# Second MoE of a fused attention and MoE kernel: three slots on the first weight buffer, two weight splits moved to VectorE, two products ahead of the next transposes

## The chip, the cores and the metric

The kernel runs on one core of a Trainium2 chip. The core has five engines, each with its own instruction queue that it works through in order: TensorE (PE) for matrix products, with its weight loads shown apart as PEld, VectorE (DVE), ScalarE (ACT), GpSimd (POOL) and SyncE (SP), which here issues most of the transfers. The engines wait for one another through semaphores. The metric is the time of one execution on the device, in microseconds (us).

## The reference

Three layers follow each other: an attention over 2 x 8 heads of 768 tokens, a dense two-layer network with a leaky activation, and a routed mixture of eight experts, which is the part that the change touches:

```
logits = x @ w_gate + modality_bias[modality_id]      # 1536 tokens, 512 wide, 8 experts
e_idx = np.argmax(logits, axis=1)
gate_w = probs[np.arange(N), e_idx]                   # softmax of logits at e_idx
for e in range(E):
    mask = e_idx == e
    if not mask.any():
        continue
    h = np.maximum(x[mask] @ w1[e], 0.0)              # 512 -> 1024
    out[mask] = gate_w[mask, None] * (h @ w2[e])      # 1024 -> 512
```

Each token goes through one expert only, and which one is known only when the layer before is done.

## The kernel before, in words

The attention and the first network run under a planner that records the operations and issues them in an order of its own; they fill the first 410 us or so. The second MoE, from `first()` on (line 1205), is issued in the order in which the code is written.

**Slots.** The tokens are sorted by expert into tiles of at most 128, called slots. There can be up to 19 slots; the kernel runs as many as are needed. The slots of one expert stand together. The first expert is the one with most tokens in the first two thirds, chosen early (`early_route`, with its weights fetched early), and the others follow by number. `exi` holds, for each slot, the expert and a flag that says whether new weights are needed.

**Weights.** One expert's weights are 4 MB in eight chunks: 0 to 3 are w1, 4 to 7 are w2. A chunk of 512 KB comes into one of seven `raw` tiles by a transfer that SyncE issues (`fetch_w`), and is then split into a rounded part, copied by ScalarE, and the rest, subtracted by VectorE (`split_w`, line 976; chunks 4 and 7 of slot 0 have the rest taken on GpSimd, line 1208 and 1218). Products use three of the four pairs of parts, so each is three matmuls. There are two weight buffers `mw`. `buf(t)` (line 960) gives slot 0 and slot 1 the first, slot 2 the second, and so on by turns. A slot needs new weights if its expert differs from that of the slot that had the same buffer two slots earlier; slot 2 is always the first in its buffer, so its flag is always set. For slot 1, whose expert may differ from slot 0's though they share the buffer, `other_weights_1` (line 1282) holds a conditional block that reloads the buffer in halves through small tiles `z`.

**The order of a slot.** `mm1(t, c)` is the first layer for a quarter of the columns (twelve matmuls, then a ReLU copy `hs` on ScalarE); `h_T(t, c)` transposes `hs` on TensorE and splits it into `ht` (ScalarE, then VectorE); `mm2(t, c)` is the second layer for the same quarter (six matmuls); `x_T(t)` transposes a slot's gathered rows `xg` and splits them into `xs`. After the fourth `mm2`, VectorE scales the result to `y` and GpSimd scatters it. `period(t)` runs a slot with the last two `mm2` of the slot before mixed in, and with conditional blocks (`split_if`) that split the next slot's chunks, each followed by the fetch of as many chunks further ahead (`fetch_more`).

**Routing.** `first()` runs slot 0 with the routing steps between: `route_a` (before it) builds, on VectorE, the one-hot tables `ma` and `mj`; `route_b` multiplies them on TensorE and gives `gidx`, by which GpSimd gathers the rows of slots 1 and 2; `route_c` and `route_d` give `exi`. The two halves of slot 1's conditional block then stand on either side of `mm2(0, 3)`.

Of the kernel before, what the change touches and what calls it, by code (L numbers as in the profile page):

```python
# [17 lines left out]
ALU = mybir.AluOpType  # L18
# [263 lines left out]
def tile_kernel(  # L282
# [5 lines left out]
    nc = tc.nc  # L288
    plan = Plan(tc)
    V, S, G, T, Y = (  # L290
        plan.engine(e, c) for e, c in ((nc.vector, "D"), (nc.scalar, "A"), (nc.gpsimd, "G"), (nc.tensor, "P"), (nc.sync, "S"))
    )
# [3 lines left out]
    E = w_gate.shape[1]  # L296
# [26 lines left out]
    def bank(pool, tag):  # L323
        return pool.tile([P, 512], F32, tag=tag, name=tag)
# [441 lines left out]
    NS = NTT + E  # L766
# [42 lines left out]
    exi = const.tile([P, 2 * NS + 2], I32, name="exi")  # L809
# [99 lines left out]
    def route_b():  # L909
        mj = rt["mj"]  # L910
        sp = bank(ps_a, "a")
        for t in range(NTT):
            T.matmul(out=sp[:, 0:NS], lhsT=mas[t], rhs=mj[:, t], start=(t == 0), stop=(t == NTT - 1))
        V.tensor_scalar(out=gidx, in0=sp[:, 0:NS], scalar1=-1.0, scalar2=0.0, op0=ALU.add, op1=ALU.max)
        fetch_x(1, gidx[:, 1:2])
        fetch_x(2, gidx[:, 2:3])
        rt["sp"] = sp
# [18 lines left out]
    def route_d():  # L936
        exs, ns, be, sp = (rt[n] for n in ("exs", "ns", "be", "sp"))
        V.tensor_scalar(out=exs[:, 1], in0=colf[:, 0:NS], scalar1=ns, scalar2=esf, op0=ALU.is_lt, op1=ALU.mult)
        V.scalar_tensor_tensor(out=exs[:, 0], in0=colf[:, 0:NS], scalar=ns, in1=exs[:, 0], op0=ALU.is_ge, op1=ALU.mult)
        V.tensor_tensor(out=exs[:, 0], in0=exs[:, 0], in1=exs[:, 1], op=ALU.add)  # L940
        V.tensor_scalar(out=exi[:, 0:NS], in0=exs[:, 0], scalar1=float(E - 1), scalar2=None, op0=ALU.min)
        V.memset(exs[:, 2, 0:3], 1.0)
        V.tensor_tensor(out=exs[:, 2, 1:2], in0=exs[:, 0, 1:2], in1=exs[:, 0, 0:1], op=ALU.not_equal)
        V.tensor_tensor(out=exs[:, 2, 3:], in0=exs[:, 0, 3:], in1=exs[:, 0, 1:NS - 2], op=ALU.not_equal)

        V.scalar_tensor_tensor(out=exi[:, NS:2 * NS], in0=colf[:, 0:NS], scalar=be[:, 1, E - 1:E], in1=exs[:, 2], op0=ALU.is_lt, op1=ALU.mult)
        V.tensor_copy(out=exi[:, 2 * NS:2 * NS + 1], in_=be[:, 1, E - 1:E])
        sidf = lt.tile([P, NS], F32, name="sidf")
        V.tensor_scalar(out=sidf, in0=sp[:, 0:NS], scalar1=0.5, scalar2=float(4 * NT), op0=ALU.is_lt, op1=ALU.mult)
        V.scalar_tensor_tensor(out=sidx, in0=sp[:, 0:NS], scalar=-1.0, in1=sidf, op0=ALU.add, op1=ALU.add)  # L950


    EN_SP = [mybir.EngineType.SP]
    EN_AV = [mybir.EngineType.Activation, mybir.EngineType.DVE]
# [3 lines left out]
    raw_of = {}  # L958

    def buf(t):  # L960
        return 0 if t == 0 else (t - 1) % 2

    def fetch_w(t, e, cond, c):
        raw = rawt[nraw[0] % len(rawt)]
# [11 lines left out]
    def split_w(t, chunks, eng=V):  # L976
        for c in chunks:
            raw, hl = raw_of.pop((t, c)), mw[buf(t)][c]
            S.activation(out=hl[:, 0], in_=raw, func=ACTF.Copy)
            eng.tensor_tensor(out=hl[:, 1], in0=raw, in1=hl[:, 0].bitcast(F32), op=ALU.subtract)  # L980
# [8 lines left out]
    def spl(dst, src):  # L989
        S.activation(out=dst[:, 0], in_=src, func=ACTF.Copy)  # L990
        V.tensor_tensor(out=dst[:, 1], in0=src, in1=dst[:, 0].bitcast(F32), op=ALU.subtract)
# [166 lines left out]
    def mm1(t, c):  # L1158
        hp = bank(ps_h, "h")
        xt = xs_t[t % 2]  # L1160
        wv = mw[buf(t)][c].rearrange("p t (k f) -> p t k f", k=KD)
        n = 0
        for kk in range(KD):
            for xa, wa in P3:
                T.matmul(out=hp[:, 0:QW], lhsT=xt[:, xa, kk, :], rhs=wv[:, wa, kk, :], start=(n == 0), stop=(n == 3 * KD - 1))
                n += 1
        hs = gp.tile([P, QW], F32, tag="t", name="hs")
        S.activation(out=hs, in_=hp[:, 0:QW], func=ACTF.Relu)
        sl[t, "h", c] = hs

    def h_T(t, c):
        hs = sl.pop((t, "h", c))
        tp = bank(ps_a, "a").rearrange("p (a c) -> p a c", a=KD)
        for a in range(2):
            T.transpose(tp[:, a], hs[:, a * P:(a + 1) * P], ident)
        ht = gp.tile([P, 2, 2, P], F32R, tag="g", name="ht")
        spl(ht, tp[:, 0:2])
        sl[t, "ht", c] = ht

    def mm2(t, c):  # L1180
        if c == 0:
            sl[t, "y"] = bank(ps_acc, "acc")
        ht, yp = sl.pop((t, "ht", c)), sl[t, "y"]
        wv = mw[buf(t)][4 + c].rearrange("p t (k f) -> p t k f", k=2)
        for k2 in range(2):
            for j, (ha, wa) in enumerate(P3):
                T.matmul(
                    out=yp, lhsT=ht[:, ha, k2, :], rhs=wv[:, wa, k2, :],
                    start=(c == 0 and k2 == 0 and j == 0), stop=(c == 3 and k2 == 1 and j == 2),
                )  # L1190
        if c == 3:
            y = p2.tile([P, DM], F32, tag="y", name="y", bufs=2)
            V.tensor_scalar(out=y, in0=sl.pop((t, "y")), scalar1=gcol[:, t:t + 1], scalar2=None, op0=ALU.mult)
            G.indirect_dma_start(
                out=out, out_offset=bass.IndirectOffsetOnAxis(ap=sidx[:, t:t + 1], axis=0), in_=y, in_offset=None,
                bounds_check=NT - 1, oob_is_err=False,
            )

    def next_x(u):
        if u < NS - 1:  # L1200
            x_T(u)
        if u + 1 < NS - 1:
            fetch_x(u + 1, gidx[:, u + 1:u + 2])

    def first():
        mm1(0, 0)
        mm1(0, 1)
        split_w(0, [4], G)
        h_T(0, 0)
        split_w(0, [5])  # L1210
        mm1(0, 2)
        h_T(0, 1)
        mm1(0, 3)
        route_b()
        split_w(0, [6])
        mm2(0, 0)
        h_T(0, 2)
        split_w(0, [7], G)
        route_c()
        mm2(0, 1)  # L1220
        h_T(0, 3)
        route_d()
        x_T(1)
        mm2(0, 2)
        other_weights_1(range(4))
        mm2(0, 3)
        other_weights_1(range(4, 8))
        fetch_more(7)

    def period(t, lagged):  # L1230

        u = t + 1
        mm1(t, 0)
        if lagged:
            mm2(t - 1, 2)
        next_x(u)
        split_if(t, [6])
        mm1(t, 1)
        h_T(t, 0)
        split_if(t, [7])  # L1240
        split_if(u, [0])
        if lagged:
            mm2(t - 1, 3)
        mm1(t, 2)
        h_T(t, 1)
        split_if(u, [1, 2])
        mm2(t, 0)
        mm1(t, 3)
        h_T(t, 2)
        split_if(u, [3, 4])  # L1250
        mm2(t, 1)
        h_T(t, 3)
        split_if(u, [5])

    def drain(t):
        mm2(t, 2)
        mm2(t, 3)

    fq = [(u, c) for u in range(2, NS - 1) for c in range(8)]
    regs = {}  # L1260

    def fetch_more(n):
# [9 lines left out]
            fetch_w(u, *regs[u], c)  # L1272

    def split_if(u, chunks):
        if not 2 <= u < NS - 1:
            return
        need = nc.values_load(exi[0:1, NS + u:NS + u + 1], engines=EN_AV, min_val=0, max_val=1)  # L1277
        with tc.If(need > 0):
            split_w(u, chunks)
        fetch_more(len(chunks))  # L1280

    def other_weights_1(chunks):

        e = nc.values_load(exi[0:1, 1:2], engines=EN_SP, min_val=0, max_val=E - 1)
        need = nc.values_load(exi[0:1, NS + 1:NS + 2], engines=EN_AV + EN_SP, min_val=0, max_val=1)
        with tc.If(need > 0):  # L1286
            for c in chunks:
                for j in range(2):
                    z = p2.tile([P, 512], F32, tag="y", name="z", bufs=2)
                    if c < 4:  # L1290
                        Y.dma_start(out=z.rearrange("p (e k f) -> p e k f", e=1, k=2), in_=w1v[:, ds(e, 1), 2 * j:2 * j + 2, c * QW:(c + 1) * QW])
                    else:
                        Y.dma_start(out=z.rearrange("p (e d) -> p e d", e=1), in_=w2v[:, ds(e, 1), 2 * (c - 4) + j, :])
                    hl = mw[0][c][:, :, j * 512:(j + 1) * 512]
                    S.activation(out=hl[:, 0], in_=z, func=ACTF.Copy)
                    V.tensor_tensor(out=hl[:, 1], in0=z, in1=hl[:, 0].bitcast(F32), op=ALU.subtract)
# [9 lines left out]
    e = nc.values_load(exi[0:1, 2 * NS + 1:2 * NS + 2], engines=EN_SP, min_val=0, max_val=E - 1)  # L1306
# [48 lines left out]
```

## Time and profile before

| | us |
|---|---|
| median of three runs | 627.63 |
| lowest and highest | 626.22, 629.51 |
| the profiled execution, device time | 628.37 |
| its span in the trace | 626.6 |
| TensorE busy | 571.8 (91%) |
| VectorE busy | 388.4 (62%) |
| ScalarE busy | 307.2 (49%) |
| GpSimd busy | 214.7 (34%) |

The span is the time from the first to the last recorded instruction; the device time has a little more around it. A row of a timeline gives the start, the length of the merged run of equal instructions, the engine, what is written and what is read, how many, and in square brackets the idle time of the engine before it with what ended it. Line L70 is the helper that issues every operation outside the planner, so rows are told apart by tile names: h is mm1's result, acc mm2's, and a the one that all transposes and small products share. The ends of matmuls are modelled and overlap a little; in the chain of waits the overlaps are taken out.

### The profile page before, as it was taken

The numbers are of one execution on the slowest core, as the hardware profiler recorded it, in microseconds if no ns is written. First come the engines' busy times: TensorE is split into PE (matmuls) and PEld (weight loads), VectorE is DVE, ScalarE is ACT, GpSimd is POOL, SyncE is SP. The second block draws the span as 40 slices with busy tenths as digits, with TensorE's granted clock in tenths as the row PEclk, the third lists the DMA queues.
The fourth block names the chain that finished last, engine by engine and source line by source line (L and its number), as shares of the span: only waits on it lengthen the run. The fifth ranks groups of instructions, "written<-read, shape, count | busy, mean of one in ns | idle before, by whom it ended". The sixth has DMA issues, their size and how long they took to land. (4 is left out here: it accounts for less than half of the span.)

```text
span 626.6 us, 13126 instructions
## 1 busy us (share of the span) xinstructions
PE 571.8 (91%) x4476; PEld 511.5 (82%) x4476; DVE 388.4 (62%) x1005; ACT 307.2 (49%) x653; POOL 214.7 (34%) x221
## 2 busy tenths in 40 slices
PE   4568798999979999999999999997699999999995
PEld 3457687888869898998998999886599999998994
DVE  7899889878547777777322433878452249982221
ACT  3765667767535454453332343543442258872231
POOL 3445547355125456465322222215011211121120
PEclk9868879999979999999999999999899999999999
DMA  9897999896423233222000000552811199941111
GB/s 185 181 197 150 215 188 182 152 177 110 89 72 82 88 102 102 72 96 68 1 2 2 34 35 35 190 169 80 299 40 34 53 317 336 360 171 51 36 53 34
DMA packets 119856, 75.82 MB, mean 121 GB/s; under 512 B 87355, under 2 KB 107863, under 8 KB 119768
## 3 DMA queue, kind: packets, MB, share of 16 engines
q1 hardware_dynamic: 117208, 67.14, 42.5%
q0 software_dynamic: 2560, 7.64, 3.9%
q8 instruction: 39, 0.64, 0.4%
q14 instruction: 49, 0.40, 0.2%
HBM read 97.08 MB, written 7.30 MB: 167 GB/s over the span
## 5 line engine op out<-in xcount | busy, mean ns | idle before, releaser
L153 PE MATMUL h<-xT,w 128*128 128x256 f32 x888 | 117.6, 288 | 1.9 <-ACT xT L153 1.5
L153 PEld LDWEIGHTS h<-xT,w 128*128 128x128 f32 x888 | 113.6, 194 | 5.1 <-ACT xT L153 1.7
L153 PE MATMUL acc<-w,g 128*128 128x512 f32 x432 | 110.7, 404 | 4.2 <-ACTq L1090 4.2
L70 PE MATMUL h<-mw,xs 128*128 128x256 f32 x720 | 99.2, 287 | 0.4 <-DVEq L1286 0.4
L153 POOL TENSOR_TENSOR g<-t,g 128x256 fp32r<-128x256 f32 x74 | 65.0, 881 | 98.8 <-ACT g L153 58.2
L70 PE MATMUL acc<-mw,ht 128*128 128x512 f32 x360 | 96.8, 406 | 0.3 <-DVE ht L70 0.3
L153 PEld LDWEIGHTS acc<-w,g 128*128 128x128 f32 x432 | 80.3, 193 | 20.4 <-ACTq L1090 4.5
L70 PEld LDWEIGHTS h<-mw,xs 128*128 128x128 f32 x720 | 92.6, 192 | 3.4 <-DVEq L1286 0.7
L70 PEld LDWEIGHTS acc<-mw,ht 128*128 128x128 f32 x360 | 63.5, 188 | 12.0 <-DVE ht L70 0.8
L70 POOL DMA_INDIRECT out<-y,sidx x15 | 18.4, 1225 | 152.7 <-DVE y L70 138.2
L70 DVE TENSOR_TENSOR mw<-raw,mw 128x1024 fp32r<-128x1024 f32 x46 | 55.4, 1224 | 14.8 <-ACT mw L70 13.8
L153 DVE SCALAR_TENSOR_TENSOR t<-t,alpha_sb,h 128x256 f32<-128x256 f32 x74 | 35.2, 477 | 45.2 <-ACT t L153 45.1
L153 POOL TENSOR_TENSOR w<-dx,w 128x512 fp32r<-128x512 f32 x32 | 43.6, 1361 | 53.0 <-ACT w L153 50.1
L70 ACT ACTIVATE hs<-h 128x256 f32<-128x256 f32 x60 | 22.8, 380 | 68.5 <-PE h L70 61.0
L70 ACT ACTIVATE mw<-raw 128x1024 fp32r<-128x1024 f32 x48 | 49.6, 1055 | 13.9 <-DMA raw<-in_moe_w 10.2
L153 DVE SCALAR_TENSOR_TENSOR dx<-wraw,dx 128x512 uint32<-128x512 uint32 x64 | 53.3, 837 | 0.4
L70 DVE TENSOR_TENSOR ht<-a,ht 128x256 fp32r<-128x256 f32 x60 | 25.2, 421 | 45.4 <-ACT ht L70 45.4
L153 ACT ACTIVATE t<-h 128x256 f32<-128x256 f32 x74 | 28.0, 381 | 43.8 <-PE h L153 42.0
L153 ACT ACTIVATE g<-t 128x256 fp32r<-128x256 f32 x74 | 30.8, 418 | 36.4 <-DVE t L153 31.3
L153 ACT ACTIVATE sp<-sp,mn 128x256 f32<-128x256 f32 (+1 forms) x96 | 39.4, 479 | 15.7 <-DVE mn L153 15.7
L153 PE MATMUL a<-vring,pth 128*128 128x64 bf16 (+1 forms) x880 | 36.2, 203 | 8.1 <-DMA pth<-pl 6.8
L153 PEld LDWEIGHTS <-pth 128*128 128x128 f16 x880 | 32.5, 104 | 12.5 <-DMA pth<-pl 7.7
(167 smaller groups left out, 835.0 us busy)
## 6 DMA issues: line engine op xcount, KB each, us to landing
raw<-in_moe_w SPq DMA_DIRECT2D x125, 512.0 KB
wraw<-in_moe_w_in SPq DMA_DIRECT2D x16, 512.0 KB
wraw<-in_moe_w_out SPq DMA_DIRECT2D x16, 512.0 KB
xs<-x SPq DMA_DIRECT2D x12, 258.0 KB
kr<-in_k SPq DMA_DIRECT2D x12, 256.0 KB
qr<-in_q SPq DMA_DIRECT2D x12, 256.0 KB
vr<-in_v SPq DMA_DIRECT2D x12, 256.0 KB
vring<-vglob SPq DMA_DIRECT2D x8, 96.5 KB
```

The source lines that it names most:

```text
L70: return method(*a, **kw)
L153: call = lambda: method(*a, **kw)
```

## The change

Slots 0, 1 and 2 have the first buffer, and later slots take the second and the first by turns. `route_d` sets the flags to fit: slots 1 and 2 are compared with the slot just before, slot 3 is always flagged, later ones are compared two slots back. `other_weights` now takes the slot as an argument, and its two halves for slot 2 stand at the end of `period(1)` and, in `period(2)`, behind `mm2(1, 3)`. The queue of fetches and the splits begin with slot 3. In `first()` the subtractions for chunks 4 and 7 are on VectorE, and `mm2(0, 2)`, which is two products of three matmuls each, stands ahead of `route_d` and `x_T(1)`.

```diff
-        V.memset(exs[:, 2, 0:3], 1.0)
-        V.tensor_tensor(out=exs[:, 2, 1:2], in0=exs[:, 0, 1:2], in1=exs[:, 0, 0:1], op=ALU.not_equal)
-        V.tensor_tensor(out=exs[:, 2, 3:], in0=exs[:, 0, 3:], in1=exs[:, 0, 1:NS - 2], op=ALU.not_equal)
+        V.memset(exs[:, 2, 0:4], 1.0)
+        V.tensor_tensor(out=exs[:, 2, 1:3], in0=exs[:, 0, 1:3], in1=exs[:, 0, 0:2], op=ALU.not_equal)
+        V.tensor_tensor(out=exs[:, 2, 4:], in0=exs[:, 0, 4:], in1=exs[:, 0, 2:NS - 2], op=ALU.not_equal)
...
     def buf(t):
-        return 0 if t == 0 else (t - 1) % 2
+        return 0 if t < 3 else t % 2
...
     def first():
         mm1(0, 0)
         mm1(0, 1)
-        split_w(0, [4], G)
+        split_w(0, [4])
         h_T(0, 0)
...
-        split_w(0, [7], G)
+        split_w(0, [7])
         route_c()
         mm2(0, 1)
         h_T(0, 3)
+        mm2(0, 2)
         route_d()
         x_T(1)
-        mm2(0, 2)
-        other_weights_1(range(4))
+        other_weights(1, range(4))
         mm2(0, 3)
-        other_weights_1(range(4, 8))
+        other_weights(1, range(4, 8))
         fetch_more(7)
...
     def period(t, lagged):
...
         if lagged:
             mm2(t - 1, 3)
+            if t == 2:
+                other_weights(2, range(4, 8))
...
         split_if(u, [5])
+        if t == 1:
+            other_weights(2, range(4))
...
-    fq = [(u, c) for u in range(2, NS - 1) for c in range(8)]
+    fq = [(u, c) for u in range(3, NS - 1) for c in range(8)]
...
     def split_if(u, chunks):
-        if not 2 <= u < NS - 1:
+        if not 3 <= u < NS - 1:
             return
...
-    def other_weights_1(chunks):
+    def other_weights(t, chunks):
-        e = nc.values_load(exi[0:1, 1:2], engines=EN_SP, min_val=0, max_val=E - 1)
-        need = nc.values_load(exi[0:1, NS + 1:NS + 2], engines=EN_AV + EN_SP, min_val=0, max_val=1)
+        e = nc.values_load(exi[0:1, t:t + 1], engines=EN_SP, min_val=0, max_val=E - 1)
+        need = nc.values_load(exi[0:1, NS + t:NS + t + 1], engines=EN_AV + EN_SP, min_val=0, max_val=1)
```

How the queues change is seen at three places. The first is VectorE in the routing, from mj on; mw_4 to mw_7 are the rests of slot 0's w2 chunks, and pre, be, nst and ex are route_c's. Before:

```order
L70 TENSOR_TENSOR mj<-jrel,jf 128x240
L70 TENSOR_TENSOR ht<-a,ht 128x256
L70 TENSOR_TENSOR mw_5_6979<-raw_5964,mw_5_6979 128x1024
L70 TENSOR_TENSOR ht<-a,ht 128x256
L70 TENSOR_SCALAR gidx<-a 128x20
L70 TENSOR_TENSOR mw_6_6980<-raw_5962,mw_6_6980 128x1024
L70 TENSOR_TENSOR ht<-a,ht 128x256
L70 TENSOR_TENSOR pre<-before,tl 128x64
```

On the same engine at the same place after the change:

```order
L70 TENSOR_TENSOR mj<-jrel,jf 128x240
L70 TENSOR_TENSOR mw_4_6978<-raw_5963,mw_4_6978 128x1024
L70 TENSOR_TENSOR ht<-a,ht 128x256
L70 TENSOR_TENSOR mw_5_6979<-raw_5964,mw_5_6979 128x1024
L70 TENSOR_TENSOR ht<-a,ht 128x256
L70 TENSOR_SCALAR gidx<-a 128x20
L70 TENSOR_TENSOR mw_6_6980<-raw_5962,mw_6_6980 128x1024
L70 TENSOR_TENSOR ht<-a,ht 128x256
L70 TENSOR_TENSOR mw_7_6981<-raw_6982,mw_7_6981 128x1024
L70 TENSOR_TENSOR pre<-before,tl 128x64
```

Two subtractions have come in, one ahead of the first ht and so of gidx, one ahead of route_c and so of exi.

The second place is ScalarE behind slot 1's first transposes; hs and ht belong to slot 1, and mw_0 to mw_2 with numbers from 6986 on are slot 2's chunks in the second buffer. Before:

```order
L70 ACTIVATE hs<-h 128x256
L70 ACTIVATE ht<-a 128x256
L1277 TENSOR_LOAD exi
L1277 ISA x2
L1278 COMPARE_AND_BRANCH
L70 ACTIVATE mw_0_6986<-raw_6983 128x1024
L1278 UNCONDITIONAL_BRANCH x2
L70 ACTIVATE hs<-h 128x256
L70 ACTIVATE ht<-a 128x256
```

On ScalarE there after the change, up to the block that now stands ahead of slot 2 (z are the small tiles of the reload):

```order
L70 ACTIVATE hs<-h 128x256
L70 ACTIVATE ht<-a 128x256
L70 ACTIVATE hs<-h 128x256
L70 ACTIVATE ht<-a 128x256
L70 ACTIVATE hs<-h 128x256
L70 ACTIVATE ht<-a 128x256 x2
L1289 TENSOR_LOAD exi
L1290 COMPARE_AND_BRANCH
L70 ACTIVATE mw_0_5956<-z 128x512 x2
```

The weight copies between slot 1's own copies are gone, and the conditional block for slot 2 stands behind slot 1's last ht.

The third place is VectorE in slot 2 after the change; y is slot 1's result, mw_0_6986 the first chunk of slot 3, and the block at L1289 the second half of slot 2's:

```order
L70 TENSOR_TENSOR ht<-a,ht 128x256
L1281 TENSOR_LOAD exi
L1282 COMPARE_AND_BRANCH
L70 TENSOR_TENSOR mw_0_6986<-raw_6983,mw_0_6986 128x1024
L1282 UNCONDITIONAL_BRANCH x2
L70 TENSOR_SCALAR y<-acc,gcol 128x512
L1289 TENSOR_LOAD exi
L1290 COMPARE_AND_BRANCH
L70 TENSOR_TENSOR mw_4_6978<-z,mw_4_6978 128x512 x2
```

The block that guards the w2 half of the first buffer stands behind y, and y behind a split.

## Rows read from the trace of the kernel before

**Rows 1.** Stretches: us, each engine's busy us (instructions), TensorE clock, DMA share, GB/s.

```profile
430.00:460.00 30.00, 22.63 (x138) 19.74 (x139) 17.22 (x31) 13.40 (x22) 5.22 (x4) 0.94 0.54 180
450.00:453.00 3.00, 1.84 (x9) 1.85 (x10) 2.72 (x4) 2.74 (x5) 0.00 (x0) 0.62 1.00 367
460.00:490.00 30.00, 30.00 (x201) 27.18 (x200) 8.38 (x18) 8.01 (x22) 5.95 (x6) 1.00 0.16 51
```

**Rows 2.** Chain that ended last, around 440 to 458: start, length, what.

```profile
440.16 9.59 DMA raw<-in_moe_w
...
451.84 2.49 PE h L70 x12
...
456.18 1.43 PE h L70 x12
457.61 0.22 PE a L70 x2
457.83 1.39 PE acc L70 x6
```

**Rows 3.** Timeline of TensorE, 424 to 452: start, length, what, idle before.

```profile
424.85 0.46 PE L70 MATMUL a<-mj,ma 128*128 128x20 f16 x12 [1.39 <-DVE mj L70]
...
431.08 0.63 PE L70 MATMUL a<-ident,xg 128*128 128x128 f32 x4 [2.43 <-DMA xg<-xs,gidx]
...
435.04 1.55 PE L70 MATMUL h<-mw,xs 128*128 128x256 f32 x11 [0.42 <-DVEq L1286]
...
441.51 1.58 PE L70 MATMUL h<-mw,xs 128*128 128x256 f32 x12
444.38 0.44 PE L70 MATMUL a<-ident,hs 128*128 128x128 f32 x2 [1.29 <-ACT hs L70]
...
451.16 0.69 PE L70 MATMUL a<-ident,hs 128*128 128x128 f32 x2 [4.26 <-ACT hs L70]
```

**Rows 4.** Timeline of ScalarE, at slot 2's first weight chunk.

```profile
442.99 1.06 ACT L70 ACTIVATE mw<-raw 128x1024 fp32r<-128x1024 f32 x1 [3.83 <-DMA raw<-in_moe_w]
```

**Rows 5.** Tile raw alone, 461 to 509: us, VectorE, ScalarE, GpSimd busy, clock, DMA.

```profile
461.00:509.00 48.00, 0.00 (x0) 0.00 (x0) 0.00 (x0) 1.00 0.29 90
```

**Rows 6.** Timeline of GpSimd in the routing.

```profile
421.68 2.43 POOL L70 TENSOR_TENSOR mw<-raw,mw 128x1024 fp32r<-128x1024 f32 x1 [10.37 <-ACT mw L70]
426.95 1.70 POOL L70 DMA_INDIRECT xg<-xs,gidx  x1 [2.83 <-DVE gidx L70]
...
429.91 2.38 POOL L70 TENSOR_TENSOR mw<-raw,mw 128x1024 fp32r<-128x1024 f32 x1
```

**Rows 7.** Timeline of VectorE in the routing.

```profile
421.01 3.18 DVE L70 TENSOR_SCALAR ma<-colf,rmod,tok 128x128 f16<-128x128 f32 x4
...
425.04 1.22 DVE L70 TENSOR_TENSOR mw<-raw,mw 128x1024 fp32r<-128x1024 f32 x1
...
426.51 0.17 DVE L70 TENSOR_SCALAR gidx<-a 128x20 int32<-128x20 f32 x1
...
429.63 2.71 DVE L70 TENSOR_SCALAR exs<-colf,nst,esf 128x20 f32<-128x20 f32 x1
```

**Rows 8.** Tile ma over the whole run: duration ns min/median/max, first and last start.

```profile
L70 DVE TENSOR_SCALAR ma<-colf,rmod,tok x12: 337/341/2408, 397.5 to 421.8; 128x128 f16<-128x128 f32 x12
```

**Rows 9.** VectorE's queue at slot 1's two conditional blocks: durations, first and last start.

```profile
L1285 DVEq TENSOR_LOAD <-exi x2: 302/310/317, 434.0 to 435.4; - x2
L1286 DVEq EVENT_SEMAPHORE  x2: 21/21/21, 435.0 to 436.2; - x2
```

**Rows 10.** Timeline of all engines, at the last transposes of a later slot.

```profile
465.16 0.38 PE L70 MATMUL a<-ident,hs 128*128 128x128 f32 x2
...
466.00 0.42 DVE L70 TENSOR_TENSOR ht<-a,ht 128x256 fp32r<-128x256 f32 x1 [1.08 <-ACT ht L70]
```

**Rows 11.** Timeline of all engines, in a slot with weight splits.

```profile
507.84 0.38 PE L70 MATMUL a<-ident,hs 128*128 128x128 f32 x2
...
512.00 0.74 DVE L70 TENSOR_SCALAR y<-acc,gcol 128x512 f32<-128x512 f32 x1
```

## The prediction

> **What bounds the kernel now.** I read the table of stretches first, then the chain that ended last, then each engine's timeline around the one weak place. In [rows 1] the reader is to see that from 460 us on TensorE is busy 30.00 of 30 us at full clock, while from 430 to 460 us it is busy 22.63 us. So nothing after 460 can be gained by a change that removes no matmul, and this one removes none; the question is how early that full stretch begins. The chain [rows 2] has a single piece there that is not work: 9.59 us in which a weight chunk is under way, ending where ScalarE copies it at 449.77. Everything after it is matmul.
>
> TensorE's timeline [rows 3] shows the waits one by one: 1.39 us for the routing one-hot mj, 2.43 us for slot 1's gathered rows, 0.42 us for VectorE's passing a conditional block (L1286), then 1.29 and 4.26 us for ScalarE's hs. ScalarE is not slow there: it stands in its own queue before the copy of slot 2's first weight chunks, which are still in flight [rows 4], and the hs copies and transposed halves of slot 1 are queued behind. [...]
>
> **Part 1: slot 2 in buffer 0, fetches begin with slot 3.** Fifteen slots ran, and no weight chunk was split between 461 and 509 us [rows 5]: slot 3 needed nothing new against slot 1, which had the same buffer. Slots lie expert by expert, so slot 2 between them has slot 1's expert too. Before, slot 2 had the other buffer, and 4 MB had to come all the same; now its block is jumped over, and the 4 MB are wanted one slot later. What goes: all splits during slot 1, hence ScalarE's wait for the chunks. I compare the stretch from the end of slot 1's last first-layer product to the end of slot 2's first. It was 442.94 (441.51 [rows 3] + 1.43) to 454.33 (451.84 + 2.49 [rows 2]), 11.39 us. The work in it at full clock is a transpose pair 0.22, six matmuls 1.39, a pair 0.22, twelve matmuls 1.43 [rows 2], in sum 3.26. So 8.13 us go. The chunks are as long under way as before, some 10 us, but are first wanted about a slot later; eight splits beside one slot's products are what TensorE's unbroken stretch already covers, with the same seven chunks fetched ahead. I cost that at nothing; if the cover failed, the old 4.26 us wait would be back one slot later.
>
> **Part 2: two late splits from GpSimd to VectorE.** GpSimd took 2.43 and 2.38 us for them [rows 6]. In the same microseconds two VectorE rows are far too long [rows 7]: four ma operations 3.18 us, where one takes 0.341 in the median [rows 8], and a 20-element exs operation 2.71 us, which ends at 432.34 just after GpSimd's split (432.29). I take the waits as the splits' doing: 3.18 - 4 x 0.34 = 1.82 and 2.71 - 0.34 = 2.37, in sum 4.19 us that go from VectorE. Added are two splits at about 1.22 us [rows 7], one ahead of ht(0,0), one ahead of route_c, 2.44 us. VectorE's operations stand back to back from ma to exi, so this is a plain sum: 1.75 us earlier at the block's end, where TensorE was let go at 435.04 [rows 3]; now 433.3. On the way gidx comes 0.6 us earlier (-1.82 + 1.22), and with it the gather and slot 1's rows (431.08, now 430.5), in time for that.
>
> **Part 3: mm2(0,2) ahead of x_T(1).** Its six matmuls (1.39 us) go into the wait for the rows. Left behind x_T(1), with rows at 430.5, the two products (2.8 us), the transposes and the first matmul of slot 1 would last till about 434.1, 0.8 us past the new release. So the move is needed for part 2 to count, and brings nothing on top. It issues no DMA and passes only route_d on VectorE's side, which doesn't read it.
>
> **Part 4: the added wait.** other_weights(2) writes buffer 0, so TensorE's reads of it in slot 2 must wait till ScalarE and VectorE have passed the blocks, run or not. From a load of the flag on VectorE to the signal behind the jump it took 1.0 us the first time and 0.8 the second [rows 9]; the load begins when the operation ahead is let go.
> First block: ahead of it on VectorE is ht(1,3), which starts 0.84 us after its transposes (465.16 to 466.00, [rows 10]). Transposes at t, then: release at t + 0.84 + 0.8 to 1.0, while the second matmul of slot 2 is wanted at t + 0.22 + 0.12. It waits 1.3 to 1.5 us; I take 1.4. Nothing lies between, so nothing hides it.
> Second block: ahead is y of slot 1, behind a split. In a slot with splits y starts 4.16 us after the slot's first transposes [rows 11] (507.84 to 512.00), so the release comes 4.96 to 5.16 us after them; the second matmul of mm2(2,0) is wanted after 0.22 + 1.39 + 1.43 + 0.22 + 0.23 = 3.49. It waits 1.5 to 1.7; I take 1.6. Behind the blocks stand slot 3's xs, and ht(2,1) with the splits of chunks 1 and 2: none is wanted within 2 us. y also waits till SyncE is past the first block, behind seven weight issues made in slot 1; it has slot 2's first half to spare.
> Bounds, for no row shows these two jumps: ht(1,3) itself can't be hidden, so the first costs at least 0.84 + 0.42 - 0.34 = 0.9; the second can cost nothing, if y comes sooner than beside a full stream of weights. From above, a jump could have to fetch code; the nearest row is a small transfer, 2.43 us from the gather's end (428.65, [rows 6]) to the rows' arrival [rows 3], on each. I keep to the rows of like jumps.
> [...]
>
> The memset of four elements for three and the shifted widths of two comparisons stay operations of a few elements; I cost them at nothing.
>
> **Sum.** 1.75 + 8.13 - 1.4 - 1.6 = 6.9 us. The profiled execution took 628.37 us with a span of 626.6; after it, a span of 619.7 and 621.5 us. It lies 0.74 above the median of 627.63, so I forecast 627.63 - 6.9 = **620.8 us**.
>
> **Rivals.**
> *The new waits are hidden.* VectorE in slot 2 has less to do than in a full weight stream, so the second block may be passed in time, and the first at its floor of 0.9: gain 9.0, 618.6 us; with TensorE's three waits in the routing (4.24 us, [rows 3]) all gone besides, 616.2. For it: slot 1 has no splits at all now. Against: the split of slot 3's first chunk still stands ahead of y.
> *VectorE's long rows are not GpSimd's doing.* Then part 2 only adds 2.44 us in place of taking 1.75: gain 2.7, 625.0 us. Against: both long rows, of unlike operations, end as GpSimd's splits end, and the median ma of twelve took 0.341 us.
> *Each jump fetches code.* The two waits grow by 2.43 us each: gain 2.0, 625.6 us. Against: like jumps took 0.8 and 1.0 us, and TensorE runs unbroken through the jumps of every later slot [rows 1]. [...]
> *Slower: slot 2's block runs.* If slot 2 had another expert than slot 1, 4 MB would come in sixteen halves through two small tiles with TensorE standing: at the 367 GB/s of [rows 1] at least 11.4 us, without overlap, so 627.6 - 6.9 + 11.4 = 632 or more. It decides as soon as the first expert has fewer than three slots. [rows 5] speaks against it.
>
> **How the numbers follow.** Forecast 0.68 (its own range 619.0 to 622.5), hidden waits 0.16, not GpSimd 0.06, code fetch 0.06, block runs 0.02, something unseen 0.02. The range of 617.2 to 624.2 takes in the first two and the bounds of the waits and leaves out the rest. About 0.5% (3.1 us) is what a measurement of this kernel can tell from no change: faster 0.85, same 0.12, slower 0.03.
>
> **What would show it.** ScalarE's weight copies must be missing from slot 1 and return in slot 2; the four ma and exs must be back under 0.4 us each, with no weight subtraction on GpSimd in these slots; TensorE must wait about 1.4 us for VectorE ahead of slot 2's second matmul and about 1.6 us within mm2(2,0), at granted clock 1.00, and not again up to the last slots. Wrong would be: a wait for a weight chunk in slots 2 or 3, z transfers, or a wait over 3 us at a jump.

## The result and the profile after

The changed kernel takes 621.68 us in the median of four runs (620.04 to 622.10), beside 627.91 us for the kernel before on the same chip (626.22 to 629.51). The ratio (of the means, as in the table below) is 0.9896, 95% interval 0.9865 to 0.9928: 1.0% faster. The forecast was 620.8 us with a range of 617.2 to 624.2. The profiled execution has a span of 619.6 us; the forecast from the profiled one of before was 619.7.

VectorE's four late ma operations began between 418.09 us (e4 below) and 421.51 us (e9), behind code that no kernel here changes. So for a sum to half a microsecond the executions are compared from a landmark: from these four ma to the last scatter on GpSimd. Each kernel has one profiled execution, and so one landmark; how far it varies is seen where a kernel was profiled again (e10, e11). In the kernel before the first is at 421.01 [rows 7], the second is this row of GpSimd's timeline, 199.54 us later:

```profile
620.55 1.01 POOL L70 DMA_INDIRECT out<-y,sidx  x1 [10.35 <-DVEq L1319]
```

VectorE's timeline of the changed kernel, which answers to [rows 7]; ht here is slot 1's last, y slot 1's result:

```profile
420.35 1.12 DVE L70 TENSOR_SCALAR ma<-colf,rmod,tok 128x128 f16<-128x128 f32 x4
...
421.97 1.22 DVE L70 TENSOR_TENSOR mw<-raw,mw 128x1024 fp32r<-128x1024 f32 x1
...
429.17 0.28 DVE L70 TENSOR_SCALAR exs<-colf,nst,esf 128x20 f32<-128x20 f32 x1
...
442.41 0.42 DVE L70 TENSOR_TENSOR ht<-a,ht 128x256 fp32r<-128x256 f32 x1 [1.08 <-ACT ht L70]
...
449.93 1.23 DVE L70 TENSOR_TENSOR mw<-raw,mw 128x1024 fp32r<-128x1024 f32 x1 [0.80 <-ACTq L1290]
452.58 0.75 DVE L70 TENSOR_SCALAR y<-acc,gcol 128x512 f32<-128x512 f32 x1 [1.43 <-SPq L1290]
```

The ma and exs rows are short, and the split of chunk 4 stands on VectorE. New is the bracket of the last row: y waited 1.43 us for SyncE's queue at the block, although the split ahead had ended at 451.16.

GpSimd's last row in the same execution, 192.79 us behind the ma, so 6.75 us less than before:

```profile
613.14 1.01 POOL L70 DMA_INDIRECT out<-y,sidx  x1 [10.30 <-DVEq L1323]
```

TensorE's timeline of the changed kernel, which answers to [rows 3]:

```profile
422.64 0.46 PE L70 MATMUL a<-mj,ma 128*128 128x20 f16 x12
...
429.50 0.63 PE L70 MATMUL a<-ident,xg 128*128 128x128 f32 x4 [1.51 <-DMA xg<-xs,gidx]
...
432.08 1.54 PE L70 MATMUL h<-mw,xs 128*128 128x256 f32 x11 [0.44 <-DVEq L1290]
...
438.54 1.58 PE L70 MATMUL h<-mw,xs 128*128 128x256 f32 x12
439.95 0.38 PE L70 MATMUL a<-ident,hs 128*128 128x128 f32 x2
...
441.58 0.38 PE L70 MATMUL a<-ident,hs 128*128 128x128 f32 x2
442.57 2.09 PE L70 MATMUL h<-mw,xs 128*128 128x256 f32 x12 [0.61 <-ACTq L1290]
444.50 1.56 PE L70 MATMUL acc<-mw,ht 128*128 128x512 f32 x6
...
450.79 0.38 PE L70 MATMUL a<-ident,hs 128*128 128x128 f32 x2
450.93 0.48 PE L70 MATMUL acc<-mw,ht 128*128 128x512 f32 x1
453.44 1.42 PE L70 MATMUL acc<-mw,ht 128*128 128x512 f32 x5 [2.04 <-DVEq L1290]
454.70 1.59 PE L70 MATMUL h<-mw,xs 128*128 128x256 f32 x12
```

The waits for mj and for hs are gone; the rows' wait is down to 1.51 us; two waits at slot 2's block have come (L1290, the line of slot 1's blocks too, which is why the 0.44 us wait has it as well), the second the longest left. Of the first wait the bracket shows only 0.61 us, up to ScalarE's signal; the rest, up to VectorE's, lies within the row, whose twelve matmuls take 2.09 us for 1.43 of work. In the stretches that answer to [rows 1] the granted clock is 1.00 throughout, and TensorE is busy 26.77 of 30 us where it was 22.63:

```profile
430.00:460.00 30.00, 26.77 (x179) 23.67 (x178) 12.79 (x28) 12.81 (x25) 5.08 (x5) 1.00 0.56 189
450.00:453.00 3.00, 1.40 (x12) 1.09 (x10) 1.57 (x2) 1.79 (x4) 0.00 (x0) 1.00 0.05 20
460.00:490.00 30.00, 30.00 (x202) 27.14 (x201) 11.86 (x22) 10.60 (x25) 3.96 (x4) 1.00 0.13 37
```

### The profile page after: what moved, and what is told of

Read it like the earlier page. It is cut to its first block, busy times and chain, and to the rows that moved or that the text cites. A ratio compares the mean times of both kernels' runs of the same rounds, so it can differ in the third digit from the quotient of the medians.

```text
span 619.6 us, 13087 instructions
## 1 busy us (share of the span) xinstructions
PE 570.9 (92%) x4476; PEld 509.9 (82%) x4476; DVE 385.3 (62%) x1007; ACT 307.4 (50%) x653; POOL 211.1 (34%) x219
## 5 line engine op out<-in xcount | busy, mean ns | idle before, releaser
L70 PEld LDWEIGHTS h<-mw,xs 128*128 128x128 f32 x720 | 91.2, 188 | 4.6 <-DVEq L1290 1.0
L70 DVE TENSOR_TENSOR mw<-raw,mw 128x1024 fp32r<-128x1024 f32 x48 | 57.6, 1223 | 8.2 <-ACT mw L70 6.5
```

Source lines behind the costliest of these rows:

```text
L70: return method(*a, **kw)
```

## The experiments

Eleven kernels were run. "Landmark" is the time from the late ma to the last scatter in the profiled execution (before 199.54, changed 192.79), with the starts of the two in brackets; the ratio is to the kernel before on the same chip.

| | landmark us | median us | ratio, 95% interval |
|---|---|---|---|
| e1 sharing alone | 194.72 (419.58, 614.30) | 621.89 | 0.9918, 0.9902 to 0.9933 |
| e2 splits on VectorE alone | 197.69 (420.00, 617.69) | 625.54 | 0.9974, 0.9954 to 0.9995 |
| e3 products moved alone | 199.65 (420.57, 620.22) | 626.20 | 0.9994, 0.9974 to 1.0014 |
| e4 changed, no blocks for slot 2 | 189.23 (418.09, 607.32) | 617.38 | 0.9852, 0.9835 to 0.9869 |
| e5 changed, fetches behind the block | 191.28 (420.32, 611.60) | 620.58 | 0.9905, 0.9874 to 0.9936 |
| e6 changed, block waits filled | 189.22 (419.36, 608.58) | 617.55 | 0.9868, 0.9845 to 0.9890 |
| e7 changed, products not moved | 193.49 (419.50, 612.99) | 620.94 | 0.9920, 0.9892 to 0.9949 |
| e8 changed, one split on GpSimd | 192.66 (419.73, 612.39) | 620.94 | 0.9909, 0.9880 to 0.9937 |
| e9 as e6, products not moved | 189.90 (421.51, 611.41) | 618.98 | 0.9878, 0.9852 to 0.9904 |
| e10 changed, again | 191.29 (419.12, 610.41) | 619.15 | 0.9895, 0.9869 to 0.9920 |
| e11 as e6, again | 189.19 (418.98, 608.17) | 617.32 | 0.9857, 0.9831 to 0.9883 |

From e4 on the landmarks lie 1 to 3 us further below that of the kernel before than the medians lie below its median on the same chip. The kernel before has one landmark only, so the differences among the changed versions are safer than those from it.

**e1, sharing alone.** The changed kernel with three lines taken back:

```diff
-        split_w(0, [4])
+        split_w(0, [4], G)
-        split_w(0, [7])
+        split_w(0, [7], G)
-        mm2(0, 2)
         route_d()
         x_T(1)
+        mm2(0, 2)
```

> Part 1 alone: slots 0 to 2 on the first buffer with the two blocks for slot 2, GpSimd splits and the place of mm2(0,2) as in the kernel before. Theory (the parts add up): the weight-chunk waits of slot 1 go (8.1 us), the two block waits come (1.3 and 2.3 us in the changed kernel's trace), so 4.5 us less than before, about 623.4 us; ma and exs stay at 3.2 and 2.7 us. Rival (the sharing is the whole of it and the routing's 1.75 us is hidden behind something else): as the changed kernel, 621.7 us.

The landmark is 4.8 us shorter than before, for 4.5 expected. VectorE's timeline shows the two long rows again, as expected:

```profile
419.58 3.18 DVE L70 TENSOR_SCALAR ma<-colf,rmod,tok 128x128 f16<-128x128 f32 x4
...
428.20 2.70 DVE L70 TENSOR_SCALAR exs<-colf,nst,esf 128x20 f32<-128x20 f32 x1
```

and TensorE's shows slot 1's first product let go 14.02 us behind the ma, as in the kernel before (14.03):

```profile
433.60 1.53 PE L70 MATMUL h<-mw,xs 128*128 128x256 f32 x11 [0.48 <-DVEq L1290]
```

So by these two profiled executions the sharing is some 70% of the gain, and the rest is the routing's. That is against the rival by the landmark (194.72, not 192.79); the medians, taken on different chips, do not tell them apart (621.89 and 621.68).

**e2, the splits alone.** The kernel before with

```diff
-        split_w(0, [4], G)
+        split_w(0, [4])
-        split_w(0, [7], G)
+        split_w(0, [7])
```

> Part 2 alone: both late splits on VectorE, buffers and order as before. Theory (the long VectorE rows are GpSimd's splits' doing): ma back to 0.34 us each, exs under 0.4, the release of slot 1's first product 1.0 to 1.7 us earlier, and as the chunk fetches of slot 2 hang on exi they come earlier by as much: 626.2 to 626.9 us. Rival 1 (the long rows have another cause): they stay and two splits of 1.22 us come on top, 630.3 us. Rival 2 (the chunk wait gives the gain back, because the transfers are bound elsewhere): same as before, 627.9 us, with the 4.26 us wait grown by 1 to 1.7.

The landmark is 1.85 us shorter and the median 1.2 us lower. Both long rows are gone, against the first rival. From VectorE's timeline:

```profile
420.00 1.12 DVE L70 TENSOR_SCALAR ma<-colf,rmod,tok 128x128 f16<-128x128 f32 x4
...
428.82 0.29 DVE L70 TENSOR_SCALAR exs<-colf,nst,esf 128x20 f32<-128x20 f32 x1
```

One expectation missed: slot 1's first product began 13.75 us behind the ma, only 0.28 us sooner than before, in place of 1.0 to 1.7. VectorE had passed the block (its y behind it waited 2.37 us for TensorE, to 434.00), but TensorE was not ready. It had waited 2.87 us for the rows, its granted clock had fallen to 0.50, and the two products behind x_T(1) took 4.04 us. The gain came later, at the chunks: TensorE waited 3.79 us for hs in place of 1.29 + 4.26, against the second rival, by which that wait would have grown.

```profile
429.12 1.09 PE L70 MATMUL a<-ident,xg 128*128 128x128 f32 x4 [2.87 <-DMA xg<-xs,gidx]
...
433.75 1.58 PE L70 MATMUL h<-mw,xs 128*128 128x256 f32 x12
...
447.23 0.69 PE L70 MATMUL a<-ident,hs 128*128 128x128 f32 x2 [3.79 <-ACT hs L70]
...
429.00:432.00 3.00, 2.88 (x9) 2.52 (x10) 2.18 (x13) 0.60 (x1) 0.00 (x0) 0.50 0.22 77
```

**e3, the move alone.** The kernel before with mm2(0, 2) ahead of route_d() and x_T(1).

> Part 3 alone: mm2(0,2) ahead of route_d and x_T(1), all else as before. Theory: the release of slot 1 is VectorE's, at the end of the exi chain, so TensorE's wait for the rows shrinks by 1.4 us and the wait at the block grows by as much: no change, 627.9 us. Rival (TensorE's own work between the rows and slot 1 is the bound): 1.4 us less, 626.5 us.

No change (199.65 against 199.54). TensorE's timeline shows why: the wait for the rows falls from 2.43 to 1.13 us, waits at GpSimd's split and at the block take its place, and slot 1's product is let go 14.01 us behind the ma (434.58 - 420.57), as before (14.03).

```profile
430.70 0.63 PE L70 MATMUL a<-ident,xg 128*128 128x128 f32 x4 [1.13 <-DMA xg<-xs,gidx]
431.89 1.42 PE L70 MATMUL acc<-mw,ht 128*128 128x512 f32 x5 [0.33 <-POOL mw L70]
433.65 0.38 PE L70 MATMUL h<-mw,xs 128*128 128x256 f32 x1 [0.34 <-ACTq L1286]
434.58 1.56 PE L70 MATMUL h<-mw,xs 128*128 128x256 f32 x11 [0.55 <-DVEq L1286]
```

**e4, no blocks for slot 2.** The changed kernel with

```diff
-            if t == 2:
-                other_weights(2, range(4, 8))
...
-        if t == 1:
-            other_weights(2, range(4))
```

> The changed kernel without slot 2's two conditional blocks, which leaves out the reload of the first buffer for a slot 2 whose expert differs from slot 1's (here it does not). Theory: TensorE's two waits at the blocks (1.3 and 2.3 us) are the blocks' price and go: 3.6 us less than the changed kernel, about 618.1 us, span about 616.0. Rival (they hide a wait for slot 3's chunks or for VectorE that comes due at once): 620 to 621.7 us, with a new wait in slots 2 or 3.

This kernel leaves out the reload that slot 2 would need if its expert were not slot 1's. It takes 3.56 us less than the changed kernel on the landmark. In its table of stretches TensorE has no wait left from 430 us on:

```profile
430.00:460.00 30.00, 30.00 (x212) 27.63 (x212) 16.33 (x25) 16.25 (x30) 5.58 (x5) 1.00 0.55 185
```

The two waits (1.27 and 2.30 us, below) are the whole difference: no later wait came due.

**e5, the fetches behind the first block.**

```diff
         other_weights(1, range(4, 8))
-        fetch_more(7)
...
         if t == 1:
             other_weights(2, range(4))
+            fetch_more(7)
```

> The changed kernel with slot 3's first seven chunk fetches issued behind slot 2's first block in place of ahead of it. In the changed kernel y of slot 1 waited 1.43 us for SyncE, whose eight signals behind the jump came one by one from 445.9 to 452.4 us while the chunks landed. Theory (behind the jump SyncE signs for the transfers left out only after the weight transfers issued before have landed): the signals come at once, y starts as soon as VectorE's split ends, TensorE's wait in mm2(2,0) shrinks from 2.0 to about 0.8 us; from the late ma to the last scatter 191.4 us against 192.8 in the changed kernel. Rival (SyncE is late because it has seven issues to make, or y is bound by VectorE): unchanged, 192.8 us.

191.28 us, as expected. SyncE's eight signals behind the jump, by windows of its queue at line L1290: in the changed kernel they come singly, over 6.5 us,

```profile
L1290 SPq EVENT_SEMAPHORE  x1: 17/17/17, 445.9 to 445.9; - x1
...
L1290 SPq EVENT_SEMAPHORE  x1: 17/17/17, 448.5 to 448.5; - x1
...
L1290 SPq EVENT_SEMAPHORE  x1: 17/17/17, 449.7 to 449.7; - x1
...
L1290 SPq EVENT_SEMAPHORE  x1: 17/17/17, 451.1 to 451.1; - x1
...
L1290 SPq EVENT_SEMAPHORE  x2: 17/17/17, 452.4 to 452.4; - x2
```

and in e5 all eight within 0.9 us:

```profile
L1290 SPq EVENT_SEMAPHORE  x8: 3/15/665, 436.1 to 437.0; - x8
```

The trace's semaphore events say what SyncE waits for. Each of the first seven signals stands in for a left-out transfer of z and waits on a semaphore that one of the seven chunk transfers also raises, in sixteen parts. In the changed kernel the sixteenth parts of the last four chunks came at 448.44, 449.73, 451.05 and 452.35 us, and the signals 0.01 to 0.02 us behind each. So a signal waits for the chunk transfer that shares its semaphore; in e5 none was under way. In e5 y follows the split at once and TensorE's wait within mm2(2,0) is

```profile
451.90 1.42 PE L70 MATMUL acc<-mw,ht 128*128 128x512 f32 x5 [0.55 <-DVEq L1290]
```

The medians show no gain from this step alone: the ratio is 0.9905, that of the changed kernel 0.9896, and e10 below shows the changed kernel itself with y not held and a landmark of 191.29.

**e6, the waits filled.** Slot 1's last two products stand between the blocks, and the fetches behind both; period(2) runs without products of slot 1.

```diff
         other_weights(1, range(4, 8))
-        fetch_more(7)
...
-            if t == 2:
-                other_weights(2, range(4, 8))
...
         if t == 1:
             other_weights(2, range(4))
+            drain(1)
+            other_weights(2, range(4, 8))
+            fetch_more(7)
...
-            period(t, t > 1)
+            period(t, t > 2)
```

> A version of the changed kernel in which slot 1's last two products stand ahead of slot 2's first: behind h_T(1,3) come the first block, mm2(1,2), mm2(1,3) with y, the second block, and only then the fetches; slot 2 then runs without products of slot 1 mixed in. Nothing is left out. Theory: TensorE has 2.8 us of products to do while the blocks are passed, and SyncE has no transfer to wait for, so both waits go: from the late ma to the last scatter 189.2 us, as without the blocks, about 3.6 us less than the changed kernel. Rival (unmixed, slot 2 has new waits, for ht behind its transposes or for the later chunks): 190.5 to 193 us.

189.22 us, as without the blocks: this is the best version found, with all that the changed kernel computes, and 1.3% below the kernel before. The late fetches alone (e5) leave 2.06 us more than this: the first block's 1.27 us and 0.8 us at the second, which the two products fill here. From 431 us on TensorE is busy to within 0.11 us:

```profile
431.00:460.00 29.00, 28.89 (x200) 26.56 (x201) 15.00 (x23) 15.65 (x30) 4.95 (x5) 1.00 0.56 192
```

**e7, the products not moved.** The changed kernel with mm2(0, 2) back behind x_T(1).

> The changed kernel with mm2(0,2) back behind x_T(1). Theory (once VectorE's chain is shorter, TensorE's own work behind the gathered rows becomes the bound): the release of slot 1's first product is followed at once or comes late, and the run is 0.8 us longer: from the late ma to the last scatter 193.6 us. Rival (VectorE's chain is the bound with or without it): 192.8 us, and the wait at the block shorter by what the wait for the rows is longer.

0.70 us longer, for 0.8 expected, but not in the way expected. TensorE waited 2.85 us for the rows, and the clock fell:

```profile
428.61 1.09 PE L70 MATMUL a<-ident,xg 128*128 128x128 f32 x4 [2.85 <-DMA xg<-xs,gidx]
429.35 4.25 PE L70 MATMUL acc<-mw,ht 128*128 128x512 f32 x12
433.43 1.58 PE L70 MATMUL h<-mw,xs 128*128 128x256 f32 x12
...
443.93 2.09 PE L70 MATMUL h<-mw,xs 128*128 128x256 f32 x12 [0.61 <-ACTq L1290]
...
453.28 1.43 PE L70 MATMUL acc<-mw,ht 128*128 128x512 f32 x5 [0.53 <-DVEq L1290]
```

Slot 2's first product began 24.43 us behind the ma (443.93 - 419.50) in place of 22.22 (442.57 - 420.35), so 2.2 us late; 1.5 us came back at the second block, where the chunks had landed in time and y did not wait. So the 0.70 us is the sum of two unforeseen things; beside e10, where y did not wait either, e7 is 2.2 us longer. The granted clock was 0.60 on the mean of this stretch, where e2's above had 0.50 and the changed kernel 1.00:

```profile
428.00:431.00 3.00, 2.39 (x8) 2.13 (x9) 2.56 (x15) 0.60 (x1) 0.00 (x0) 0.60 0.32 88
```

**e8, one split on GpSimd.** The changed kernel with split_w(0, [4], G).

> The changed kernel with only the first of the two splits (chunk 4) back on GpSimd. Theory (a GpSimd split holds up the VectorE operation that falls into it): the four ma take 3.2 us again, exs stays at 0.28 us; VectorE's chain is 1.8 - 1.2 = 0.6 us longer at the first release: from the late ma to the last scatter 193.4 us. Rival 1 (the two long rows have a common cause, such as any GpSimd split in this stretch): exs long too, about 2.7 us, and 195 us or more. Rival 2 (ma is long for a reason of its own): neither is long, 191.6 us.

The rows are as the theory has them, ma long and exs short, so each long row belongs to the split that runs beside it:

```profile
419.73 3.18 DVE L70 TENSOR_SCALAR ma<-colf,rmod,tok 128x128 f16<-128x128 f32 x4
...
429.85 0.29 DVE L70 TENSOR_SCALAR exs<-colf,nst,esf 128x20 f32<-128x20 f32 x1
```

The total is a miss: 192.66 in place of 193.4. The release came 1.4 us later (432.84 - 419.73 = 13.11, against 11.73), not 0.6, and the second block, with y not held by SyncE, gave it back. Beside e10, where y was not held either, e8 is 1.37 us longer.

```profile
432.84 1.56 PE L70 MATMUL h<-mw,xs 128*128 128x256 f32 x11 [0.55 <-DVEq L1290]
...
452.70 1.42 PE L70 MATMUL acc<-mw,ht 128*128 128x512 f32 x5 [0.54 <-DVEq L1290]
```

**e9, e6 without the move.** As e7, on e6.

> The version with the filled block waits (e6), with mm2(0,2) back behind x_T(1). With the changed kernel the same step cost only 0.7 us in all, but slot 2's first product began 2.2 us later and y's wait for SyncE was gone, which may have given 1.5 us back. Here nothing later waits. Theory (TensorE then idles 2.85 us for the rows, the granted clock falls, and the four transposes and two products run at half speed): from the late ma to the last scatter 191.4 us, 2.2 us more than with the move. Rival (the move is worth the 0.8 us of TensorE's own order, and the other chip's clock or chance made the rest): 190.0 us.

189.90: the rival holds, 0.7 us. TensorE waited 2.85 us for the rows, as in e7, but here the clock stayed at 1.00 and the two products took 3.05 us in place of 4.25:

```profile
430.64 0.63 PE L70 MATMUL a<-ident,xg 128*128 128x128 f32 x4 [2.85 <-DMA xg<-xs,gidx]
431.02 3.05 PE L70 MATMUL acc<-mw,ht 128*128 128x512 f32 x12
...
430.00:433.00 3.00, 2.36 (x13) 2.02 (x14) 2.69 (x15) 0.60 (x1) 0.00 (x0) 1.00 0.31 88
```

So the same wait can cost the clock or not; what decides it was not shown. e9's timed runs spread over 3.5 us (617.0 to 620.5), e11's beside it over 1.6. That this spread is the clock's was not shown either: the slowest of e9 is the profiled one, which kept its clock here and was late already at the ma (421.51).

**e10 and e11, the changed kernel and e6 on one chip.**

> The changed kernel itself once more, beside e11 on the same chip. Theory: 192.8 us from the late ma to the last scatter, y again held by SyncE's signals for 0.4 to 1.5 us according to when the chunks land; 1.0 to 1.1% below the kernel before.

> The version with the filled block waits (e6) once more, beside the changed kernel on the same chip. Theory: 3.6 us less than e10, 189.2 us from the late ma to the last scatter. Rival (its lead was the chip's or the call's): within 1 us of e10.

e10's landmark is 191.29, not 192.79: this time y followed the split at once, and TensorE's second wait was 0.52 us. From VectorE's and TensorE's timelines:

```profile
449.84 0.75 DVE L70 TENSOR_SCALAR y<-acc,gcol 128x512 f32<-128x512 f32 x1
...
450.70 1.43 PE L70 MATMUL acc<-mw,ht 128*128 128x512 f32 x5 [0.52 <-DVEq L1290]
```

The seven chunks had landed 14.5 us after the first issue (434.80 to 449.32) in place of 16.2 (436.19 to 452.35). The semaphore events show where the difference lies: the last chunk's first fifteen parts had landed 14.4 us after that issue in e10 and 14.6 in the changed kernel (450.80), but its sixteenth came 0.1 us behind them in e10 and 1.55 in the changed kernel. Of the five profiled executions with the fetches ahead of slot 2's block, y was held in two (the changed kernel, e1) and not in three (e7, e8, e10). e11 repeats e6 to 0.03 us. The lead of e11 over e10 is 2.1 us by the landmark and 1.8 us in the medians, against the rival; it is less than the 3.6 expected, because e10's own wait had shrunk.

## Why the prediction was right

**Sharing, -8.13 us.** From the end of slot 1's last first-layer product to the end of slot 2's first it was 11.39 us; now 439.95 to 444.50, 4.55 us, of which 1.27 is the first block's wait (441.58 to 444.50 is 2.92, less 0.22 + 1.43 of work). Without it 8.1 us went; 1.06 of it is the twelve matmuls' own, 2.49 us [rows 2] at a granted clock of 0.62 on the mean of 450 to 453 us [rows 1], and 1.43 of work at 1.00 now. e1 gives the part as a whole.

**Splits, -1.75 us.** From the ma to the release of slot 1's first product it was 435.04 - 421.01 = 14.03 us, and is 432.08 - 420.35 = 11.73: 2.3 us less. The long rows were GpSimd's doing, as predicted (e2, e8); the term was mis-sized by 0.55 us, mostly because VectorE's rows overlap their neighbours: a 1.22 us split is followed by the next operation 1.14 us after its start (421.97 to 423.11), and four ma of 0.34 take 1.12 together. That the release on TensorE needs the move as well, which the prediction said, is what e2 shows (0.28 us of it without the move).

**The move, needed for 0.8 us.** Right in size by the landmark of e9 (0.7; in the medians of e9 and e11, on one chip, it is 1.7), nothing by itself (e3). What the prediction didn't see is that a wait as long as that without the move can also bring the clock down (e2 and e7; not e9); with that the move is worth 2.2 us (e7 beside e10).

**First block, +1.4 us.** Measured 1.27. Nothing lay between to hide it, and in e6 two products did.

**Second block, +1.6 us.** Measured 2.30 in the profiled execution: from 450.79 to 454.70 are 3.91 us for 0.22 + 1.39 of work. Here a sentence of the prediction fails, that SyncE "has slot 2's first half to spare": it was the last one at the block, because it had to see the chunks land. With y not held the same place costs 0.8 us (e5: 450.74 to 453.16 less 1.61). So the mechanism behind the 1.6 was right in neither case: where y was held, the wait was SyncE's, and where it was not, y came 3.3 us after slot 2's first transposes (e10, 446.52 to 449.84) in place of the 4.16 taken from a full stream of weights, as the prediction's own bound allowed. That 1.6 stood between the two was luck.

**Sum.** 2.3 + 8.1 - 1.27 - 2.30 = 6.8 us, against 6.9 forecast and 6.75 on the landmark. The closeness is in part luck: 0.55 us too little for the splits and 0.7 too little for the second block nearly cancel, and with y not held the landmark fell by 8.25 us (e10). The median fell by 6.2 us, and by 6.8 us on e10's chip. Of the rivals, the waits were not hidden; the two jumps took 0.6 and 0.8 us on VectorE from the load of the flag to the signal (442.4 to 443.0, 452.6 to 453.4), no more than those of before (1.2 us at the second in e5, 450.6 to 451.8); slot 2's block did not run; and the long rows were GpSimd's doing.

## What to carry to other kernels

A conditional block can cost its readers a wait even when it is jumped over (1.27 and 0.8 to 2.3 us here): put work that does not read its tile between the last operation ahead of the block and the first reader, as e6 and e11 did. If the block holds transfers that share semaphores with long transfers on the same queue, issue the long ones behind it: that took away a wait which came in two of five executions and cost 1.1 to 1.5 us there, and which the medians alone don't show. And compare executions from a landmark just ahead of the change, more than one execution of each kernel: up to 3.4 us of the total came from code that was the same, and the same kernel's landmark differed by 1.5 us.

## What was not expected of the hardware

SyncE's signals behind a jumped block with eight transfers came one by one over 6.5 us, five of them 0.01 to 0.02 us behind the landing of the chunk on the same semaphore, where without transfers under way eight took 0.9 us (e5). One part in sixteen of a chunk came 1.55 us behind the others in the changed kernel, and with it the signal. And a wait of 2.85 us on TensorE brought the granted clock down to 0.60 in a stretch of 3 us in e7 (one of 2.87 us to 0.50 in e2), but left it at 1.00 in e9, as a wait of 2.43 us had in the kernel before (1.00 from 431 to 434 us).
